# A transform and an expert layer on one core: the ramp reordered, filters split, weight roundings moved, products of zeros added, pieces of the body shifted

## The chip, the cores and the metric

The kernel runs on one core of a Trainium2 chip. Its time is the device time of one execution in microseconds. A profile is one execution; its span is mostly some 2 us below that execution's time. A product of 32-bit numbers shows as two records in these traces, so x8 in a line of PE is four products. Engines are called PE (tensor engine), PEld (its weight loads), DVE (vector engine), ACT (scalar engine), POOL (GpSimd) and SP (the engine that issues most of the transfers).

## The reference

```python
X = np.fft.rfft(x, axis=1)                      # x: 8 batches x 3008 positions x 256 channels
y = np.fft.irfft(X * (filt_r + 1j * filt_i), n=3008, axis=1)
h = y.reshape(24064, 256) @ w_in                # 256 x 2048
out = (h * (1.0 / (1.0 + np.exp(-h)))) @ w_out  # 2048 x 256
```

The weights arrive as 64-bit numbers. The kernel turns them into 32-bit ones on the chip; this is what "rounding" means below: 16 of them, two to a weight pair, each some five operations of DVE, two of ACT and two of POOL, and four more POOL operations after every second one.

## The kernel before

The transform of a batch goes through DRAM twice: stage 1 (products `pa`) stores d1; six groups load t2 from it, multiply (forward, `pb`), take the filter's product on DVE, add, multiply (inverse, `pc`), and store q into d2; stage 3 (`pd`) loads t4 from d2 and makes y. The expert products then run in 48 steps per batch (`px`, `pyz`, `acc`), and between them the next batch's transform is fed in piece by piece, by a list of steps and rounds. Only batch 0's transform has nothing to hide behind: it is the ramp.

```python
def stage1(u):
    t1 = tpool.tile([128, 2, 2, C], FP32, name=f"t1_{b}_{u}", tag="t")   # two buffers
    # ... products into two banks, evacuated by DVE and ACT, stored to d1 from POOL's queue

# the ramp
for u in range(8):
    part["load_x"](u)
nc.sync.dma_start(out=d_t, in_=d_dram.ap())
weights(0)
load_filters()                       # all 12 rows per partition, 3 MB
# ... sums and stage 1, eight pieces
part["load_t2"](0)
part["load_t2"](1)
nc.sync.dma_start(out=e_t, in_=e_dram.ap())
weights(1)
weights(2)
nc.sync.dma_start(out=wi_t, in_=wi_dram.ap())
rounded(0)
rounded(1)
for g in range(NG):
    part["forward"](g)
    # ... multiply and add, two halves each
    if g > 0:
        part["inverse"](g - 1)
    if g % 2 == 0:
        weights(3 + g // 2)
    rounded(2 + g)
part["inverse"](NG - 1)
part["load_t4"](0)
rounded(8)
rounded(9)
for g in range(4):
    part["stage3"](g)
# ... the other six roundings stand in steps 0 to 5, one each
```

The body's list of pieces, for batch b:

```python
put(at - 49, 0, part["load_x"], 0)              # at = 48 * b
for u in range(8):
    put(at + u - 48, 5, part["sums"], u)        # DVE
    put(at + u - 47, 3, part["stage1"], u)
```

Of the kernel before, what the change touches and what calls it, by code (L numbers as in the profile page):

```python
# [39 lines left out]
FP32 = mybir.dt.float32  # L40
# [97 lines left out]
def kernel(  # L138
# [47 lines left out]
    w_t = cpool.tile([128, 7, 2, NJP, 128], FP32)  # L186
    warm = cpool.tile([128, 1], FP32)
    bias_t = cpool.tile([128, 1], FP32)
    x_t = [xpool.tile([128, 2, 2, C], FP32, name=f"x{i}") for i in range(2)]

    def load_filters():
        for j in range(4):
            s0, tau = slot_residue(0, 0, j), (1 if j % 2 == 0 else -1)
            for half in range(2):
                off, t = (s0, tau) if half == 0 else (94 - s0, -tau)
                for k, filt in enumerate((filt_r, filt_i)):
                    p0 = 32 * j + 16 * half
                    nc.sync.dma_start(
                        out=f_t[k][p0:p0 + 16].rearrange("p g k c -> p (g k) c"),
                        in_=bass.AP(tensor=filt.tensor, offset=filt.offset + off * C,  # L200
                                    ap=[[94 * C, 16], [t * C, 2 * NG], [1, C]]))

    flip = [0]

# [20 lines left out]
    def spectral(b):  # L225
# [5 lines left out]
        def load_x(u):  # L231


            queue = nc.sync
            if b == 0:
                queue = (nc.sync, nc.scalar)[u % 2]
                if u in (0, 2):
                    xs["y"] = ypool.tile([128, 2, HALF], FP32, name=f"x_{b}_{u}", tag="y")
                if u < 4:
                    xs[u] = xs["y"][:, u % 2, 0:1024].rearrange("p (a n) -> p a n", a=2)  # L240
                elif u < 6:
                    xs[u] = t4pool.tile([128, 2, 2 * C], FP32, name=f"x_{b}_{u}", tag="t4")
                else:
                    xs[u] = x_t[u % 2]
                (nc.vector, nc.gpsimd)[u % 2].memset(xs[u][32:64], 0.0)
            else:
                xs[u] = x_t[u % 2]
            for h in range(2):
                for r0, nr in ((0, 32), (32, N1 - 32)):
                    queue.dma_start(  # L250
                        out=xs[u][64 * h + r0:64 * h + r0 + nr],
                        in_=bass.AP(tensor=x.tensor,
                                    offset=x.offset + (b * S + 32 * r0 + 4 * u + 2 * h) * C,
                                    ap=[[32 * C, nr], [32 * N1 * C, 2], [1, 2 * C]]))
# [14 lines left out]

        def stage1(u):  # L270
            ut = us.pop(u)
            t1 = tpool.tile([128, 2, 2, C], FP32, name=f"t1_{b}_{u}", tag="t")
            ps = [bank(b, f"pa_{b}_{u}_{h}") for h in range(2)]
            for par in range(2):
                for h in range(2):
                    rows = slice(64 * h, 64 * h + N1)
                    nc.tensor.matmul(out=ps[h][64 * par:64 * par + 64], lhsT=wf_t[rows, par],  # L277
                                     rhs=ut[rows, par], start=True, stop=True)
            for h in range(2):
                evac(t1[:, h], ps[h])  # L280
            for par in range(2):
                nc.gpsimd.dma_start(  # L282
                    out=d1[par].rearrange("s p n c -> (s p) n c")[:, 4 * u:4 * u + 4, :],
                    in_=t1[64 * par:64 * par + 2 * NS].rearrange("p h n c -> p (h n) c"))
# [31 lines left out]

        def add(g, k):
            z, pt = prods[g][k]
            eng = nc.vector if b > 0 else nc.gpsimd
            eng.tensor_tensor(out=z[:, 0], in0=z[:, 0], in1=pt[:, 1], op=ALU.subtract)  # L320
            eng.tensor_tensor(out=z[:, 1], in0=z[:, 1], in1=pt[:, 0], op=ALU.add)  # L321

        def inverse(g):
# [6 lines left out]
                        nc.tensor.matmul(out=ps[i][:, k, :], lhsT=e_t[rows, g, k, ri, :],  # L330
                                         rhs=zs[k][rows, ri, :], start=(ri == 0), stop=(ri == 1))
            for i in range(2):
                qt = qpool.tile([128, 2, C], FP32, name=f"q_{b}_{g}_{i}", tag="q")
                evac(qt, ps[i])
                for p in range(2):
                    a0 = p * NS + 2 * g + 12 * i
                    queue = nc.gpsimd if b > 0 else nc.scalar
                    queue.dma_start(out=d2[a0:a0 + 2, :, :].rearrange("s n c -> n s c"),  # L338
                                    in_=qt[64 * p:64 * p + 64, :, :])

# [36 lines left out]
    def plan(b, part):  # L377

        at = STEPS * b
        put(at - 49, 0, part["load_x"], 0)  # L380
        put(at - 49, 0, part["load_x"], 1)
        for u in range(8):
            put(at + u - 48, 5, part["sums"], u)
            put(at + u - 47, 3, part["stage1"], u)
        put(at - 39, 0, part["load_t2"], 0)
        put(at - 39, 0, part["load_t2"], 1)
        for g in range(NG):
            put(at + 3 * g - 37, 3, part["forward"], g)
            put(at + 3 * g - 37, 5, part["multiply"], g, 0)
            put(at + 3 * g - 36, 1, part["multiply"], g, 1)  # L390
            put(at + 3 * g - 36, 5, part["add"], g, 0)
            put(at + 3 * g - 35, 1, part["add"], g, 1)
            put(at + 3 * g - 35, 3, part["inverse"], g)
        put(at - 18, 5, part["load_t4"], 0)
        for g, step in enumerate((-16, -12, -8, -4)):
            put(at + step, 3, part["stage3"], g)
        plan_rest(b, part)
# [216 lines left out]
    def weights(jp):  # L614
        if wide:
            load_weights(jp)

    def rounded(j):
        if wide:
            round_weights(j)  # L620
        else:
            load_exact(j)


    nc.sync.dma_start(out=wf_t, in_=wf_dram.ap())
    nc.gpsimd.memset(bias_t, -896.0)
    part = spectral(0)
    for u in range(8):
        part["load_x"](u)
    nc.sync.dma_start(out=d_t, in_=d_dram.ap())  # L630
    weights(0)
    load_filters()
    for u in range(3):
        part["sums"](u)
    for u in range(8):
# [3 lines left out]
    part["load_t2"](0)  # L639
    part["load_t2"](1)  # L640
    nc.sync.dma_start(out=e_t, in_=e_dram.ap())
    weights(1)
    weights(2)
    nc.sync.dma_start(out=wi_t, in_=wi_dram.ap())
    rounded(0)
    rounded(1)
    for g in range(NG):
        part["forward"](g)
        for k in range(2):
            part["multiply"](g, k)  # L650
        for k in range(2):
            part["add"](g, k)
        if g > 0:
            part["inverse"](g - 1)
        if g % 2 == 0:
            weights(3 + g // 2)
        rounded(2 + g)
    part["inverse"](NG - 1)
    part["load_t4"](0)
    rounded(8)  # L660
    rounded(9)
    for g in range(4):
        part["stage3"](g)
    early[0] = None
    plan_rest(0, part)
    for b in range(1, B):
        plan(b, spectral(b))
    for k in range(6):
        put(k, 1, rounded, 10 + k)
        if k in (1, 3):  # L670
            put(k, 1, weights, 6 + k // 2)

    per = len(PAIRS) * 2

    stores = (((10, 1), (10, 5)), ((19, 5), (20, 1)), ((28, 5), (29, 1)), ((34, 1), (34, 5)),
              ((42, 1), (42, 5)), ((50, 1), (51, 1)))
    for pair in range(len(pairs)):
        pending.append((NJP * pair - 2 + (5 if pair % per == 3 else 1) / ROUNDS, 100,
# [54 lines left out]
```

## Time and profile before

| | before |
|---|---|
| median of 4 runs | 2746.07 us (2745.39 to 2747.09) |
| span of the profile | 2745.5 us |
| PE busy | 2630.5 us, 96% |
| first expert product starts | 146.43 us |
| steps 1 to 5 (one rounding each) | 42.94 us |
| a batch period in the body | 326.85 us |

PE is full in the body, so a gain can come from two places: the 146 us before the first expert product, and single waits in the body. The prediction below shows the lines that say so. In such a ramp the busy shares say little; a table of landmarks (the first product of each stage) and the chain of waits between two landmarks say which resource carries each stretch.

### The profile page before, as it was taken

What the parts mean: (1) busy time and instruction counts of PE and PEld (TensorE: products, weight loads), DVE (VectorE), ACT (ScalarE), POOL (GpSimd) and SP (SyncE); (2) the same over time, 40 slices, a digit from 0 to 9 for tenths busy, and PEclk for the clock granted to TensorE, in tenths of its full rate; (3) what the DMA queues carried; (4) which work ended last, traced back from release to release, by engine and by line L of the source; (5) the groups of instructions that cost most, each with busy time, mean ns of one, the idle gap of its engine ahead of it and who ended that gap; (6) DMA issues with size and microseconds to landing.
All of it is one profiled execution on the core that took longest, in us unless ns stands there. A gap on an engine that the chain in (4) does not pass through costs nothing.

```text
span 2745.5 us, 45764 instructions
## 1 busy us (share of the span) xinstructions
PE 2630.5 (96%) x17664; PEld 2198.8 (80%) x17664; DVE 1652.4 (60%) x3492; ACT 1098.9 (40%) x2994; POOL 506.0 (18%) x738
## 2 busy tenths in 40 slices
PE   2489999999999999999999999999999999999998
PEld 0368889788887888878887888878888788898987
DVE  3676655666556665666656665566655666555555
ACT  1244344433444334443444434444344433444443
POOL 2541210211111111112111121022111211110100
PEclk9789999999999999999999999999999999999999
DMA  9643221331214221332113312133121421110000
GB/s 176 192 125 79 49 46 32 88 79 40 46 37 105 65 50 23 71 85 68 35 33 82 81 47 44 35 82 85 39 47 31 107 65 43 32 27 20 9 16 15
DMA packets 187929, 166.94 MB, mean 61 GB/s; under 512 B 122176, under 2 KB 155584, under 8 KB 187456
## 3 DMA queue, kind: packets, MB, share of 16 engines
q1 hardware_dynamic: 165912, 111.89, 18.0%
q0 software_dynamic: 16256, 47.20, 6.8%
q10 hardware_dynamic: 5544, 4.93, 0.8%
q8 instruction: 138, 2.26, 0.3%
q14 instruction: 79, 0.65, 0.1%
HBM read 88.96 MB, written 74.97 MB: 60 GB/s over the span
## 4 chain that ended last, share of the span: by engine, by line
PE 90%; DVE 4%; DMA 2%; ACT 1%; issue 1%; ACTq 0%; SPq 0%; POOL 0%; DVEq 0%; POOLq 0%
PE acc L495 40%; PE px L439 24%; PE pyz L439 17%; PE pc L330 3%; PE pd L358 3%; PE pa L277 2%; PE pb L300 2%; DMA d<-t 1%; DVE g L410 1%; DVE u L265 1%; DMA x<-in_x_dram 1%; ACTq L338 0%; DVE z L321 0%; DMA raw<-in_moe_w_out_dram 0%; DVE z L320 0%
## 5 line engine op out<-in xcount | busy, mean ns | idle before, releaser
L495 PE MATMUL acc<-g,w_t 128*128 128x256 f32 (+1 forms) x5376 | 1512.5, 375 | 0.4 <-DVE g L410 0.4
L495 PEld LDWEIGHTS acc<-g,w_t 128*128 128x128 f32 x5376 | 1021.9, 190 | 115.6 <-DVE g L410 0.8
L410 DVE TENSOR_TENSOR g<-pyz,abc 128x256 f32<-128x256 f32 (+1 forms) x1152 | 478.2, 415 | 569.3 <-ACT abc L460 323.0
L410 DVE TENSOR_TENSOR g<-g 128x256 f32<-128x256 f32 (+3 forms) x1152 | 611.8, 531 | 196.6 <-ACT g L443 183.4
L439 PE MATMUL px<-ty,w_t 128*128 128x256 f32 (+1 forms) x2304 | 695.4, 383 | 3.5 <-ACT abc L454 2.9
L443 ACT ACTIVATE g<-g 128x256 f32<-128x256 f32 (+1 forms) x1152 | 472.8, 410 | 244.8 <-DVE g L410 244.8
L439 PEld LDWEIGHTS px<-ty,w_t 128*128 128x128 f32 x2304 | 420.5, 190 | 128.5 <-issue 71.0
L439 PE MATMUL pyz<-y,w_t 128*128 128x256 f32 (+1 forms) x1536 | 456.3, 379 | 10.9 <-DVE g L410 10.9
L410 POOL TENSOR_TENSOR s<-s 128x256 f32<-128x256 f32 (+1 forms) x329 | 266.4, 827 | 1022.2 <-DVE s L513 999.0
L439 PEld LDWEIGHTS pyz<-y,w_t 128*128 128x128 f32 x1536 | 282.0, 189 | 58.8 <-DVE g L410 20.1
L454 ACT COPY abc<-px 128x256 f32<-128x256 f32 (+1 forms) x384 | 141.2, 368 | 373.3 <-PE px L439 373.3
L443 ACT ACTIVATE g<-px 128x256 f32<-128x256 f32 (+1 forms) x384 | 145.8, 380 | 302.1 <-PE px L439 302.1
L460 ACT COPY abc<-px 128x256 f32<-128x256 f32 (+1 forms) x384 | 142.9, 372 | 285.2 <-PE px L439 284.9
L338 POOL DMA_DIRECT2D d<-q x168 | 99.3, 598 | 713.5 <-DVE q L208 705.6
L439 PE MATMUL px<-y,w_t 128*128 128x256 f32 (+1 forms) x768 | 226.2, 376 | 1.0 <-ACT y L210 1.0
L439 PE MATMUL pyz<-ty,w_t 128*128 128x256 f32 (+1 forms) x768 | 226.7, 377 | 0.0
L439 PEld LDWEIGHTS pyz<-ty,w_t 128*128 128x128 f32 x768 | 145.2, 190 | 19.0 <-DVE g L410 2.9
L439 PEld LDWEIGHTS px<-y,w_t 128*128 128x128 f32 x768 | 144.3, 190 | 19.6 <-ACT y L210 1.1
L447 ACT COPY abc<-px 128x256 f32<-128x256 f32 (+1 forms) x384 | 134.1, 349 | 1.3 <-PE px L439 1.3
L282 POOL DMA_DIRECT2D d<-t x128 | 65.6, 516 | 332.1 <-ACT abc L460 283.7
L330 PE MATMUL pc<-z,e_t 64*128 64x256 f32 x768 | 106.0, 413 | 16.0 <-POOL z L320 13.4
L208 DVE COPY y<-pd 128x376 f32<-128x376 f32 x64 | 51.7, 808 | 100.7 <-PE pd L358 100.7
(49 smaller groups left out, 1306.9 us busy)
## 6 DMA issues: line engine op xcount, KB each, us to landing
d<-t POOLq DMA_DIRECT2D x128, 192.0 KB, 3.0
t<-d SPq DMA_DIRECT2D x96, 256.0 KB, 3.9
t<-d SPq DMA_DIRECT2D x128, 192.0 KB, 3.9
d<-q POOLq DMA_DIRECT2D x168, 128.0 KB, 2.6
out_dram<-o SPq DMA_DIRECT2D x636, 32.0 KB, 1.8
x<-in_x_dram SPq DMA_DIRECT2D x120, 128.0 KB, 3.0
x<-in_x_dram SPq DMA_DIRECT2D x120, 60.0 KB, 2.9
raw<-in_moe_w_in_dram SPq DMA_DIRECT2D x16, 256.0 KB, 4.8
```

What stands on the lines that cost most here:

```text
L277: nc.tensor.matmul(out=ps[h][64 * par:64 * par + 64], lhsT=wf_t[rows, par], rhs=ut[rows, par], start=True, stop=True)
L282: nc.gpsimd.dma_start(out=d1[par].rearrange("s p n c -> (s p) n c")[:, 4 * u:4 * u + 4, :], in_=t1[64 * par:64 * par + 2 * NS].rearrange(" ...
L330: nc.tensor.matmul(out=ps[i][:, k, :], lhsT=e_t[rows, g, k, ri, :], rhs=zs[k][rows, ri, :], start=(ri == 0), stop=(ri == 1))
L338: queue.dma_start(out=d2[a0:a0 + 2, :, :].rearrange("s n c -> n s c"), in_=qt[64 * p:64 * p + 64, :, :])
L358: nc.tensor.matmul(out=ps[h][c0:c0 + 64, cb, i, :], lhsT=t4s[g][rows, i, 128 * cb + c0:128 * cb + c0 + 64], rhs=wi_t[rows, :], start=True, ...
L410: eng.tensor_tensor(out=out, in0=in0, in1=in1, op=op)
L439: nc.tensor.matmul(out=out, lhsT=w_t[:, c, 0, jp], rhs=rhs, start=start, stop=True, skip_group_check=True)
L443: nc.scalar.activation(out=g[:, k, 0:n], in_=g[:, k, 0:n] if src is None else src, func=AFT.Silu)
L447: nc.scalar.copy(out=sums[:, 0, 0:n], in_=xo)
L454: nc.scalar.copy(out=sums[:, 1, 0:n], in_=xo)
L460: nc.scalar.copy(out=sums[:, 2, 0:n], in_=xo)
L495: nc.tensor.matmul(out=acc[pair][i][:, h, 0:n], lhsT=w_t[:, c, 1, jp], rhs=g[:, k, 0:n], start=(jp == 0 and h == 0), stop=last, skip_group ...
```

## The change

Its intent: start the groups earlier by loading only the filter rows that the first two groups need, let stage 1 run ahead on six tiles, take the roundings out of the groups' chain, keep PE's clock up with products of zeros where it would stand still, and move a few pieces of the body off a crowded spot. The core of the diff (renamings and unchanged lines cut):

```diff
-    load_filters()
+    load_filters(0, 4)
 ...
+            if b > 0 or u < 2 or u > 5:
                 t1 = tpool.tile([128, 2, 2, C], FP32, name=f"t1_{b}_{u}", tag="t")
+            elif u < 4:
+                t1 = typool.tile([128, 2, 2, C], FP32, name=f"t1_{b}_{u}", tag="ty")
+            else:
+                t1 = us["t1"][:, u - 4]
 ...
-            eng = nc.vector if b > 0 else nc.gpsimd
+            eng = nc.vector if b > 0 or (g == NG - 1 and k == 0) else nc.gpsimd
 ...                                             # q: second half from another pool (4 tiles)
+    def idle(n):                                # n products of 128x128 zeros by 128x256 zeros
+            nc.tensor.matmul(out=ps[:, 0:256], lhsT=zero_t[:, 0:128], rhs=zero_t, ...)
+    idle(10)                                    # ahead of stage 1
 ...
-    weights(1)
-    weights(2)
+    idle(26)                                    # ahead of forward(0)
     for g in range(NG):
         part["forward"](g)
+        idle(4)
+        if g == 0:
+            load_filters(4, 2 * NG)
+        if g < 3:
+            weights(1 + g)
         ...
+        if 2 <= g < NG - 1:
+            rounded(g)
         if g > 0:
             part["inverse"](g - 1)
-        if g % 2 == 0:
-            weights(3 + g // 2)
-        rounded(2 + g)
     part["inverse"](NG - 1)
+    weights(4)
     part["load_t4"](0)
-    rounded(8)
-    rounded(9)
+    idle(22)
+    for j in range(5, 9):
+        rounded(j)
+        if j == 5:
+            weights(5)
 ...
-    for k in range(6):
-        put(k, 1, rounded, 10 + k)
+    for j in range(9, NJ):                      # seven roundings in steps 0 to 5, two in step 5
+        put(*((j - 9, 1) if j < NJ - 1 else (5, 5)), rounded, j)
 ...
-        put(at - 49, 0, part["load_x"], 0)
+        put(at - 51, 0, part["load_x"], 0)
-            put(at + u - 48, 5, part["sums"], u)
+            put(at + u - (48 if u else 49), 5, part["sums"], u)
 ...                                             # last group one step later, additions of
 ...                                             # group 4 and the stores of pair 2 later
```

More of the change, by code (lines that the diff above doesn't have):

```diff
@@ L188, with load_filters @@
     bias_t = cpool.tile([128, 1], FP32)
+    zero_t = cpool.tile([128, 256], FP32)
     x_t = [xpool.tile([128, 2, 2, C], FP32, name=f"x{i}") for i in range(2)]
-    def load_filters():
+    def load_filters(first, last):
         for j in range(4):
@@ L198, in load_filters @@
                     nc.sync.dma_start(
-                        out=f_t[k][p0:p0 + 16].rearrange("p g k c -> p (g k) c"),
-                        in_=bass.AP(tensor=filt.tensor, offset=filt.offset + off * C,
-                                    ap=[[94 * C, 16], [t * C, 2 * NG], [1, C]]))
+                        out=f_t[k][p0:p0 + 16].rearrange("p g k c -> p (g k) c")[:, first:last],
+                        in_=bass.AP(tensor=filt.tensor, offset=filt.offset + (off + t * first) * C,
+                                    ap=[[94 * C, 16], [t * C, last - first], [1, C]]))
     flip = [0]
@@ L236, in load_x @@
                 queue = (nc.sync, nc.scalar)[u % 2]
+                if u == 0:
+                    us["t1"] = gpool.tile([128, 2, 2, 2, C], FP32, name="t1_g", tag="g")
                 if u in (0, 2):
@@ L271, in stage1 @@
             ut = us.pop(u)
-            t1 = tpool.tile([128, 2, 2, C], FP32, name=f"t1_{b}_{u}", tag="t")
+            if b > 0 or u < 2 or u > 5:
+                t1 = tpool.tile([128, 2, 2, C], FP32, name=f"t1_{b}_{u}", tag="t")
+            elif u < 4:
+                t1 = typool.tile([128, 2, 2, C], FP32, name=f"t1_{b}_{u}", tag="ty")
+            else:
+                t1 = us["t1"][:, u - 4]
             ps = [bank(b, f"pa_{b}_{u}_{h}") for h in range(2)]
@@ L332, in inverse @@
             for i in range(2):
-                qt = qpool.tile([128, 2, C], FP32, name=f"q_{b}_{g}_{i}", tag="q")
+                if b > 0 or i == 0:
+                    qt = qpool.tile([128, 2, C], FP32, name=f"q_{b}_{g}_{i}", tag="q")
+                else:
+                    qt = opool.tile([128, 2, C], FP32, name=f"q_{b}_{g}_{i}", tag="o")
                 evac(qt, ps[i])
@@ L336, in inverse @@
                     a0 = p * NS + 2 * g + 12 * i
-                    queue = nc.gpsimd if b > 0 else nc.scalar
+                    queue = nc.gpsimd if b > 0 or (g == NG - 1 and i == 0) else nc.scalar
                     queue.dma_start(out=d2[a0:a0 + 2, :, :].rearrange("s n c -> n s c"),
@@ L379, in plan @@
         at = STEPS * b
-        put(at - 49, 0, part["load_x"], 0)
-        put(at - 49, 0, part["load_x"], 1)
+        put(at - 51, 0, part["load_x"], 0)
+        put(at - 51, 0, part["load_x"], 1)
         for u in range(8):
-            put(at + u - 48, 5, part["sums"], u)
+            put(at + u - (48 if u else 49), 5, part["sums"], u)
             put(at + u - 47, 3, part["stage1"], u)
@@ L386, in plan @@
         put(at - 39, 0, part["load_t2"], 1)
-        for g in range(NG):
-            put(at + 3 * g - 37, 3, part["forward"], g)
-            put(at + 3 * g - 37, 5, part["multiply"], g, 0)
-            put(at + 3 * g - 36, 1, part["multiply"], g, 1)
-            put(at + 3 * g - 36, 5, part["add"], g, 0)
-            put(at + 3 * g - 35, 1, part["add"], g, 1)
-            put(at + 3 * g - 35, 3, part["inverse"], g)
+        for g, step in enumerate((-37, -34, -31, -28, -25, -21)):
+            late = 4 if g == 4 else 0
+            put(at + step, 3, part["forward"], g)
+            put(at + step, 5, part["multiply"], g, 0)
+            put(at + step + 1, 1, part["multiply"], g, 1)
+            put(at + step + 1, 5 + late, part["add"], g, 0)
+            put(at + step + 2, 1 + late, part["add"], g, 1)
+            put(at + step + (3 if late else 2), 3, part["inverse"], g)
         put(at - 18, 5, part["load_t4"], 0)
@@ L622, in rounded @@
             load_exact(j)
+    def idle(n):
+        ps = xps.tile([128, 512], FP32, name="idle", tag="x")
+        for _ in range(n):
+            nc.tensor.matmul(out=ps[:, 0:256], lhsT=zero_t[:, 0:128], rhs=zero_t, start=True, stop=True)
     nc.sync.dma_start(out=wf_t, in_=wf_dram.ap())
+    nc.vector.memset(zero_t, 0.0)
     nc.gpsimd.memset(bias_t, -896.0)
     part = spectral(0)
+    idle(10)
     for u in range(8):
@@ L641 @@
     nc.sync.dma_start(out=e_t, in_=e_dram.ap())
-    weights(1)
-    weights(2)
-    nc.sync.dma_start(out=wi_t, in_=wi_dram.ap())
     rounded(0)
     rounded(1)
+    idle(26)
     for g in range(NG):
         part["forward"](g)
+        idle(4)
+        if g == 0:
+            load_filters(4, 2 * NG)
+            nc.sync.dma_start(out=wi_t, in_=wi_dram.ap())
+        if g < 3:
+            weights(1 + g)
         for k in range(2):
@@ L667 @@
         plan(b, spectral(b))
-    for k in range(6):
-        put(k, 1, rounded, 10 + k)
-        if k in (1, 3):
-            put(k, 1, weights, 6 + k // 2)
+    for j in range(9, NJ):
+        put(*((j - 9, 1) if j < NJ - 1 else (5, 5)), rounded, j)
+        if j in (11, 13):
+            put(j - 9, 1, weights, j // 2 + 1)
     per = len(PAIRS) * 2
-    stores = (((10, 1), (10, 5)), ((19, 5), (20, 1)), ((28, 5), (29, 1)), ((34, 1), (34, 5)),
+    stores = (((10, 1), (10, 5)), ((19, 5), (20, 1)), ((30, 1), (30, 5)), ((34, 1), (34, 5)),
               ((42, 1), (42, 5)), ((50, 1), (51, 1)))
```

## The prediction

> **What bounds the kernel now.** I read the page's forty slices first, then busy time by stretch, then the chain of waits for each stretch. From the slices (68.6 us each) the reader sees that the tensor engine (PE) is full from the fourth slice on, and that the DMA engines are full only in the first:
>
> ```profile
> PE   2489999999999999999999999999999999999998
> DMA  9643221331214221332113312133121421110000
> ```
>
> So the span is a ramp (the first batch's transform, before the expert products can start), a PE-bound body, and a short tail. Busy time by stretch (length, then PE, PEld, DVE, ACT, POOL busy, then granted clock, DMA share, GB/s) splits the ramp where its work changes:
>
> ```profile
> 0.00:60.00 60.00, 18.16 (x64) 4.77 (x64) 19.35 (x31) 6.21 (x11) 11.01 (x23) 1.00 0.96 175
> 60.00:126.00 66.00, 31.04 (x288) 18.62 (x288) 42.94 (x70) 12.84 (x21) 39.06 (x55) 0.86 0.71 204
> 126.00:146.43 20.43, 8.21 (x256) 7.71 (x257) 9.45 (x15) 6.37 (x9) 9.66 (x13) 0.50 0.50 124
> 146.43:158.70 12.27, 11.16 (x30) 7.37 (x30) 9.18 (x19) 4.40 (x11) 1.41 (x2) 0.62 0.35 94
> 158.70:201.72 43.02, 38.26 (x185) 26.55 (x187) 38.53 (x69) 20.45 (x52) 24.20 (x32) 1.00 0.44 131
> ```
>
> To 60 us DMA is at 0.96 and no engine is at a third. From 60 to 126 (the six groups) nothing is full: that is a chain. From 126 to 158.7 the granted clock is at or near half. From 158.7 each step takes 8.6 us (43.02 / 5), against 7.26 us once the roundings are over. The chain of waits names what holds the first two stretches:
>
> ```profile
> 26.86 31.83 DMA d<-t x4
> ...
> 82.79 0.61 DVE q L208
> 83.42 0.67 ACTq L338
> 84.12 0.61 ACTq L338
> 84.78 0.60 ACT q L210
> 85.39 0.58 ACTq L338
> 86.02 0.62 ACTq L338
> 86.73 0.64 ACT work L579
> 87.40 0.69 DVE work L583
> ...
> 134.89 1.99 PE pd L358 x63
> ...
> 223.50 1.08 PE pd L358 x64
> ```
>
> First, the stores of stage 1: two tiles hold its output, so each evacuation waits until an earlier store has landed, and those stores share the DMA engines with 3 MB of filters. Then a loop of about 8.9 us per group: DVE's multiplications, a q copy, four store issues on ACT, and the rounding of a weight pair, whose halves hop DVE, ACT, DVE. The last two lines are the same products cold and warm: 1.99 against 1.08 us.
>
> In the body only one wait recurs. All PE waits from 200 us to the end:
>
> ```profile
> PE pyz L439 <- DVE g L410: 8.4, 12, 1.0
> ```
>
> At 813.32 the chain shows DVE with sums(0) of the next batch for 1.70 us, between the drains of a pair; PE loses 0.97 us. A batch period is 326.8 us with PE busy 325.3.
>
> [...] the clock column says 1.00 before 60 us, where stage 1's 128x512 products last 1,073 ns on average against 615 later. [...] stage-1 stores take up to 18.1 us to land while filters are queued, 2.8 us when they are not. [...] In the groups the shift of a rounding takes 0.94 us beside GpSimd's additions, 0.42 without.
>
> **The change part by part.**
>
> (a) Filters. Only 4 of 12 rows (groups 0 and 1) are loaded before t2; 2,048 of 3,072 KB move behind forward(0). While mainly filters moved, at 45 to 55 us, DMA ran at 133 to 135 GB/s: 2.1 MB / 0.134 MB per us = 15.6 us. Stage 1 also gets six tiles instead of two, so its stores are issued early; but DMA was already full, so I credit no more for that. Stage-1 stores end at 63.6 - 15.6 = 48 us. From request of t2 to full use took 5.3 us (63.66 to 68.98), so forward(0) starts at about 53 instead of 69.
>
> (b) The groups. Roundings leave groups 0, 1 and 5 and stand behind the additions in 2 to 4; q has four tiles. ACT's share then is one copy and four issues, 3.0 us, DVE's 2.4 (four products) + 0.7. The chain that made 8.9 us is gone, and what remains is what DMA must bring: the order on the queue is table e 1.57 MB, t2(2), filters 2.1 MB, weights 1, t2(3), weights 2, t2(4), weights 3, t2(5). Filters at 0.134 MB per us again 15.6 us. The rest is 1.57 + 4 x 0.52 + 3 x 1.05 + five groups' stores 2.6 = 9.4 MB; DMA ran at 242 to 273 GB/s from 85 to 95 us, so 36 us. Sum 52 us: t2(5) is in at about 100. Then forward 1.1, multiply 2.4, add 1.4 (DVE and GpSimd side by side), inverse 1.9, copy 0.7: the last q on DVE at about 107.5, before at 125.74. Gain 18.
>
> (c) From there to the first expert product: before 146.43 - 125.74 = 20.7 us. Store, landing and t4 load took 9.1 us and stay. The 22 products of zeros start about 1 us ahead of the q copy and take 9.5 us warm (0.43 each), so they end about as t4 arrives. Stage 3 then runs warm, but its third and fourth pieces still wait for a t4 tile to come free and be loaded (about 4.5 us), and four roundings at 3.4 us = 13.6 us lie on DVE. I get 18.5. Gain 2.
>
> (d) The first step runs warm: 12.3 us becomes 8.6. Gain 3.7.
>
> (e) For batch 1, sums(0) now stands ahead of step 0 in DVE's order, and its x load is issued only after the last t4 load; landing about 6 us later it blocks DVE for some 2 us. Cost 2.
>
> (f) Nine roundings stand before the steps instead of ten; the seventh in steps 0 to 5 costs 1.34 us (8.6 - 7.26), say 1.5.
>
> (g) In the body sums(0) goes a step earlier, where DVE is at 4.5 of 7.26 us. Six batches x 1.4 us = 8.4; I credit 7.5, as 1.3 us of DVE work might collide elsewhere.
>
> The other products of zeros (10 at the start, 26 before forward(0), 4 per group) lie in PE waits: 26 x 0.43 = 11 us warm, 22 cold, against a wait of some 25 us. They cost nothing and buy little, since those stretches are DMA's.
>
> Sum: 18 + 2 + 3.7 - 2 - 1.5 + 7.5 = 27.7, so 2745.9 - 27.7 = about **2718 us**.
>
> **The rivals.**
> 1. DMA doesn't bind in the groups. For it: before, rates of 359 to 370 GB/s were reached at 70 to 80 us. Then six groups at about 6 us follow from the compute side, and the last q is at 53 + 38 = 91: 16 us better, 2702.
> 2. The moved loads hurt fully: filters go slow beside t2 and the d2 stores, multiply(2) waits for all of them, and weight loads delay t2(3) to t2(5). Then the groups end near 120 and the total is about 2731. For it: [...] t2(3) now stands behind 3 MB. Against it: total bytes are unchanged.
> 3. The zeros get in the way. If PE is cold when the 22 begin, [...] any misfit with t4's arrival is added: 2 to 4 us. If they never warm it, 22 x 0.86 = 19 us delay stage 3 by 9 us: 2727.
> 4. The stall of (g) only moves: the body gives 0 instead of 7.5: about 2725.
>
> **Range and chances.** A gain over 2% needs 55 us, that is a first product at 91 us less what the body gives; the bytes that must move forbid it even under rival 1. A loss needs a new wait of 80 us. The range is rivals 1 and 2 with what the smaller terms may add: 2703 to 2731. Chances: faster 0.02, same 0.975, slower 0.005.
>
> **What would show it.** In the changed profile: the first forward product at about 53 us (above 60 proves (a) wrong); filters landing near 75 us and DMA share above 0.9 through the groups (below 0.8 favours rival 1); the last q copy at 107; stage 3's 64 products at 1.1 us instead of 1.99; the first expert product at 126; DVE waiting for x before step 0; the batch period near 325.5 and PE's 8.4 us of waits almost gone. The prediction is wrong if forward(0) doesn't come earlier, or if warm PE shortens the groups much more than the bytes allow.

## The result, and the profile after

The changed kernel takes 2723.43 us (median of 4 runs, 2719.87 to 2725.17), the one before 2746.07. The ratio is 0.9916, with a 95% interval of 0.9898 to 0.9933. Ratios here are the mean time of one kernel's runs over that of the other's of the same rounds, so they are not quite the ratio of the medians. The predicted 2718 us is 5 us off, inside its range. The profiled execution was the quickest of the four (span 2718.1 us), so the ledger below, made from the two traces, adds up to 27.4 us where the medians differ by 22.6.

The slices of the changed kernel (67.95 us each):

```profile
PE   7689999999999999999999999999999999999998
DMA  9733121421224211332122312132121421110000
```

PE fills the first slice now, but a good part of that is products of zeros, so a busy share can no longer be read as progress. Busy time by stretch, cut at the landmarks (length, then PE, PEld, DVE, ACT, POOL, granted clock, DMA share, GB/s):

```profile
0.00:42.19 42.19, 34.40 (x139) 20.17 (x140) 24.84 (x40) 8.57 (x14) 18.39 (x33) 0.88 0.90 237
42.19:60.00 17.81, 15.09 (x150) 10.04 (x150) 5.66 (x9) 0.58 (x1) 5.60 (x8) 0.90 0.92 220
60.00:80.00 20.00, 3.23 (x33) 1.25 (x34) 7.02 (x11) 1.94 (x3) 4.55 (x6) 0.57 1.05 196
80.00:104.60 24.60, 21.39 (x156) 13.57 (x156) 18.34 (x29) 4.35 (x7) 14.53 (x18) 0.86 0.72 195
104.60:127.78 23.18, 16.53 (x298) 14.57 (x297) 18.29 (x25) 8.88 (x13) 15.64 (x18) 0.78 0.77 187
127.78:138.82 11.04, 9.20 (x30) 5.84 (x30) 9.01 (x17) 3.93 (x10) 4.87 (x6) 0.84 0.25 61
```

From 60 to 80 us no engine is busy for more than 7.02 of the 20 us and DMA is full (1.05): the groups stand still for bytes. After that DMA is at 0.72. The ledger, from the landmarks of both traces (forward(0) is the start of its bulk, after both halves of t2 have landed; "last q" is the end of the last q copy on DVE; step 1 starts with the first `pa` after the first expert product, step 6 with the sixth):

| stretch | before, us | after, us | difference | predicted |
|---|---|---|---|---|
| to forward(0) | 68.98 | 42.19 | -26.8 | -16 |
| groups, to last q | 56.76 | 62.41 | +5.6 | -2 |
| to first expert product | 20.69 | 23.18 | +2.5 | -2.2 |
| step 0 | 12.28 | 11.04 | -1.2 | -1.7 |
| steps 1 to 5 | 42.94 | 47.89 | +4.9 | +1.5 |
| step 6 to stage-3 piece 4 | 21.78 | 21.78 | 0 | 0 |
| body, to the last stage-3 piece | 2336.87 | 2324.11 | -12.8 | -7.5 |
| rest | 185.2 | 185.5 | +0.3 | 0 |

The sum came out nearly as predicted, but of the six stretches for which a change was predicted only step 0 came near it. The chain of waits of the changed kernel through the groups (start, length, what):

```profile
57.68 3.87 DMA filt<-in_filt_r_dram
61.56 8.82 DMA filt<-in_filt_r_dram
70.41 7.26 DMA t<-d
...
79.76 3.71 PE idle L641 x8
83.47 1.09 PE pc L338 x8
```

The early start is paid back: group 2 waits for the filters that were moved out of the way, group 3 for a t2 that stands behind them. And four products of zeros, run cold in 3.71 us, lie on the chain ahead of an inverse product. From 77.7 to 106.7 us the chain holds no transfer any more. How much of the wait is the filters' is in the waits from 40 to 110 us (who waited for what: us in total, times, longest):

```profile
DVE z L320 <- DMA filt<-in_filt_r_dram: 17.2, 1, 17.2
```

In the body PE's waits after 200 us have shrunk from the 8.4 us that the prediction shows to the following and one more of 0.4 us, which the kernel before has too:

```profile
PE pd L369 <- DMA t<-d: 1.0, 2, 0.7
```

### The profile page after: what moved, and what is told of

It reads as the page before. It is cut to its first block, busy times and chain, and to the rows that moved or that the text cites. A ratio compares the mean times of both kernels' runs of the same rounds, so it can differ in the third digit from the quotient of the medians. Undisturbed runs are those within 1.5% of the kernel's fastest.

```text
span 2718.1 us, 46118 instructions
## 1 busy us (share of the span) xinstructions
PE 2659.3 (98%) x17828; PEld 2230.4 (82%) x17828; DVE 1655.2 (61%) x3495; ACT 1098.9 (40%) x2994; POOL 506.4 (19%) x738
## 4 chain that ended last, share of the span: by engine, by line
PE 92%; DMA 3%; DVE 2%; SPq 1%; issue 1%; ACT 1%; ACTq 0%; DVEq 0%
PE acc L508 41%; PE px L452 25%; PE pyz L452 18%; PE pc L338 3%; PE pd L369 3%; PE pa L285 2%; PE pb L308 2%; DMA t<-d 1%; DMA x<-in_x_dram 1%; DVE g L423 1%; SPq L199 1%; DMA filt<-in_filt_r_dram 0%; SPq L546 0%; DVE u L268 0%; DMA e_t<-e_tbl 0%
## 5 line engine op out<-in xcount | busy, mean ns | idle before, releaser
L452 PEld LDWEIGHTS px<-y,w_t 128*128 128x128 f32 x768 | 144.2, 190 | 22.6 <-issue 3.0
L338 PE MATMUL pc<-z,e_t 64*128 64x256 f32 x768 | 98.4, 395 | 3.5 <-POOL z L328 1.5
```

The source lines that it names most:

```text
L338: nc.tensor.matmul(out=ps[i][:, k, :], lhsT=e_t[rows, g, k, ri, :], rhs=zs[k][rows, ri, :], start=(ri == 0), stop=(ri == 1))
L452: nc.tensor.matmul(out=out, lhsT=w_t[:, c, 0, jp], rhs=rhs, start=start, stop=True, skip_group_check=True)
```

## The experiments

Twelve runs (the changed kernel again and eleven variants), all correct. The theory after reading the two traces: both the filter split and the six tiles bring forward(0) early, the bytes then hold the groups, so the real gains are the roundings' places and the body's schedule, and the rest of the change costs. The rival: the early start and the warm array are what pays. Landmarks in us from one trace each:

| run | median, us (range) | ratio to before | first forward product | last q | first expert product | steps 1 to 5 |
|---|---|---|---|---|---|---|
| before | 2746.07 | | 67.2 | 125.7 | 146.4 | 42.9 |
| after | 2723.43 (2719.87 to 2725.17) | 0.9916 | 41.2 | 104.6 | 127.8 | 47.9 |
| after again | 2722.68 (2722.32 to 2723.58) | 0.9917 | 42.1 | 105.4 | 129.6 | 45.9 |
| no zeros | 2718.47 (2717.32 to 2719.91) | 0.9902 | 42.6 | 102.3 | 126.3 | 46.6 |
| filters whole | 2716.65 (2713.68 to 2719.07) | 0.9892 | 56.5 | 101.9 | 126.2 | 46.7 |
| two tiles | 2727.89 (2725.62 to 2729.39) | 0.9935 | 48.9 | 111.0 | 135.8 | 46.0 |
| body only | 2738.50 (2736.93 to 2739.93) | 0.9977 | 66.2 | 125.7 | 147.3 | 43.0 |
| sums only | 2742.34 (2741.30 to 2745.30) | 0.9992 | 65.2 | 124.2 | 144.9 | 43.0 |
| ten roundings ahead | 2723.13 (2721.93 to 2724.16) | 0.9922 | 41.5 | 104.4 | 132.9 | 43.0 |
| reordered | 2717.41 (2716.85 to 2718.07) | 0.9900 | 40.7 | 103.5 | 125.9 | 43.0 |
| roundings as before | 2731.22 (2730.90 to 2733.43) | 0.9947 | 42.4 | 115.8 | 139.0 | 43.0 |
| no zeros in groups | 2722.34 (2721.64 to 2723.36) | 0.9914 | 42.8 | 102.3 | 128.9 | 47.9 |
| combined | 2715.83 (2714.67 to 2717.01) | 0.9889 | 56.4 | 105.9 | 126.4 | 43.1 |
| combined 2 | 2720.45 (2718.33 to 2722.09) | 0.9904 | 56.8 | 104.8 | 129.9 | 43.3 |

**The changed kernel once more.** No edit.

> The changed kernel once more, timed beside the others. Its four runs so far spread from 2719.9 to 2725.2 us with mean granted clocks of 0.989 to 0.986, while the kernel before spreads by under 2 us. If the scatter comes from how long the tensor engine runs at half clock in the ramp, the runs here should again spread over 4 to 6 us and the slower ones should show the lower mean clock; if it was one chip's chance, they should agree within 2 us. Median 2722 to 2725.

The median was as expected, the spread was not: 1.3 us here. Both chips together give 2719.9 to 2725.2, so differences under some 2 us between kernels of different calls are not used below. The clock theory of the scatter isn't borne out: this trace has a mean granted clock of 0.990 and is 3 us longer than the first, which has 0.989 (within the first four runs the slower ones did have the lower clock, 0.986 against 0.989). Single stretches scatter as well: here step 0 takes 12.39 us, not 11.04.

**Without zeros.**

```diff
-    idle(10)
-    idle(26)
-        idle(4)
-    idle(22)
```

> The changed kernel without any product of zeros (all 62 of them taken out). Prediction's view (they cost nothing and buy little): within 3 us of the changed kernel, 2720 to 2727. Rival (they are what keeps the array warm, and warm stretches are on the path): 5 to 12 us slower, 2728 to 2735, with stage 1, the forward and inverse products and stage 3 at about twice their warm durations. Second rival (they stand in the way, as the group of 22 that ends at 113.6 us, and the 4 between forward and inverse that took 3.8 us cold): 2 to 5 us faster.

The second rival is right: 4.2 us faster than the changed kernel on the same chip, with ranges that do not touch (2717.3 to 2719.9 against 2722.3 to 2723.6). The zeros do warm the array: the first stage-1 products, in the trace of the changed kernel with zeros ahead of them and then in that without:

```profile
8.29 1.68 PE L285 MATMUL pa<-u,wf_t 47*64 47x512 f32 x8 [0.67 <-DVE u L268]
```

```profile
8.33 2.58 PE L285 MATMUL pa<-u,wf_t 47*64 47x512 f32 x8 [8.33 <-DVE u L268]
```

These four products take 1.68 us behind zeros and 2.58 us without. But nothing waits for them: stage 1 is held by x, by copies and by stores (in the changed kernel, to 42 us: DVE waits 4.9 us for x, PE 1.4 for a copy, ACT and DVE 2.8 for stores), so forward(0) starts only 0.6 to 1.8 us earlier with zeros (42.2 and 43.4 against 43.9), and the last q comes 2.3 to 3.1 us later with them (104.6 and 105.4 against 102.3). The chain of the changed kernel above suggests the reason, and "no zeros in the groups" below bears it out for the last q: the four zeros stand in PE's order ahead of an inverse product, and DVE's next multiplication waits for that inverse to free its z tile (5.6 us in all; 3.9 in "no zeros in the groups"). Here warmth was worth nothing to an engine that waited anyway, and the products that made it stood in the way.

**Filters whole before t2.**

```diff
-    load_filters(0, 4)
+    load_filters(0, 2 * NG)
 ...
-            load_filters(4, 2 * NG)
```

> The changed kernel with all filter rows loaded before t2, as in the kernel before. If splitting the filters is what brings the first forward product from 67 to 41 us, it comes back to 50 to 57 us. The groups then no longer wait 17 us for filters at group 2. If the bytes bound the groups, the last q copy comes at nearly the same time as in the changed kernel (104.6 us), within 4 us, and the total is within 5 us of it (2720 to 2728). Rival: the split is worth its full 16 us in the end too: 2735 to 2740.

The idea in the title of the change, the split of the filters, costs some 6 us: without it forward(0) starts 15.6 us later (57.75 us), and still the last q is 2.7 us earlier and the kernel takes 2716.65 us against 2722.68, which is faster than the 2720 to 2728 expected. (Its four runs lie at 2714, twice, and at 2719, twice; all are faster than every run of the changed kernel, and the profile is of one at 2719.) With whole filters no wait for them is left. What holds the groups then, in two stretches of this run (columns as above):

```profile
80.00:90.00 10.00, 8.10 (x56) 5.04 (x56) 6.52 (x10) 2.02 (x4) 8.15 (x12) 0.66 0.92 269
90.00:102.00 12.00, 9.99 (x78) 6.41 (x75) 9.35 (x17) 2.41 (x4) 4.92 (x7) 0.86 0.52 147
```

To 90 us DMA (0.92, 269 GB/s) still sets the pace, then DVE's 9.35 of 12 us. The same bytes have to come in either way, and here it was better to have the filters first.

The run also shows what the tiles do, since it has six of them and the old order of loads. From 20 to 40 us, before and then in this run:

```profile
20.00:40.00 20.00, 5.17 (x22) 1.19 (x16) 3.69 (x6) 1.17 (x2) 2.01 (x4) 1.00 1.08 222
```

```profile
20.00:40.00 20.00, 17.74 (x78) 12.06 (x71) 10.65 (x18) 4.94 (x8) 10.36 (x18) 0.82 1.06 308
```

(The clock of 1.00 in the first line is no measurement: the clock records of that trace begin at 87.6 us.) The DMA share is the same, 1.08 and 1.06, but the rate is 222 against 308 GB/s, so a full share is not yet a full rate. With tiles free, the stores of stage 1 join in early and the stage is done 11.2 us sooner (forward(0) at 57.75 instead of 68.98).

**Two tiles for stage 1.**

```diff
-            if b > 0 or u < 2 or u > 5:
+            if True:                        # t1 always from the pool of two
```

> The changed kernel with stage 1 writing to two tiles again instead of six. My prediction gave the extra tiles nothing; the first forward product came 11 us earlier than predicted, so I now think they are worth about that at that point: it should start at 49 to 54 us here instead of 41. By the end of the groups part should be taken up by the shorter wait for filters: total 0 to 10 us slower, 2723 to 2733. If the tiles are worth nothing, all landmarks stay within 2 us of the changed kernel.

Forward(0) and forward(1) of this run:

```profile
48.91 1.62 PE L306 MATMUL pb<-t,d_t 64*32 64x256 f32 x32
52.39 1.09 PE L306 MATMUL pb<-t,d_t 64*32 64x256 f32 x32
```

The bulk of forward(0) (the third of its 32 records) starts at 49.45 us, where the prediction, which had credited the split of the filters alone, has 53. So the 26.8 us of the early start are 19.5 from the split (68.98 to 49.45; with up to 1.8 from the zeros) and 7.3 from the tiles (49.45 to 42.19). Taken in the other order they are 11.2 from the tiles ("filters whole") and 15.6 from the split. What DVE waits for stage-1 stores to free a tile, up to 69 us, in the kernel before, in this run, and in the run with whole filters:

```profile
DVE t L208 <- DMA d<-t: 34.7, 5, 14.5
```

```profile
DVE t L209 <- DMA d<-t: 15.0, 4, 7.9
```

```profile
DVE t L209 <- DMA d<-t: 1.7, 1, 1.7
```

At the end two tiles cost 5.2 us (2727.89 against 2722.68). Of the two ways to start early, the tiles, which let stores use a DMA rate that lay idle, keep 5.2 of their 7.3 us; the split, which only moves a load behind another use, costs more than it brings.

**The body's schedule alone**, on the kernel before.

```diff
-        put(at - 49, 0, part["load_x"], 0)      # and 1
+        put(at - 51, 0, part["load_x"], 0)      # and 1
-            put(at + u - 48, 5, part["sums"], u)
+            put(at + u - (48 if u else 49), 5, part["sums"], u)
 ...                                             # last group, additions of group 4, stores of pair 2
```

> The kernel before with only the schedule of the body changed (x loads and sums(0) earlier, the last group a step later, the additions of group 4 later, the stores of pair 2 later); ramp as before. In the changed kernel the body (from the first stage-3 piece in the steps to the last) is 12.7 us shorter than before. If that comes from the schedule alone, this runs at 2732 to 2736 us (about 0.5% faster than before). If part of it comes from the ramp (another alignment of loads), it gains only 4 to 9 us: 2737 to 2742.

The body, from the fourth piece of stage 3 to its last, takes 2324.1 us, 12.8 less than before and the same as in the changed kernel: the whole gain of the body is the schedule's. The total, 2738.5 us, misses 2732 to 2736, the range for a gain from the schedule alone, because step 0 takes 16.56 us instead of 12.28. In the waits of step 0 stands why:

```profile
DVE u L265 <- DMA x<-in_x_dram: 3.1, 1, 3.1
PE pyz L441 <- DVE g L412: 5.1, 4, 3.5
```

That is term (e) of the prediction: batch 1's x is asked for behind the last t4 load, and DVE, which needs it before step 0's drains, holds PE for 3.5 us. In the changed kernel the wait is absent: there x is requested at 123.35 us, and DVE, busy with roundings and copies, comes to it only at 129.30.

**Sums alone**, on the kernel before: `load_x` at -51 and `sums(0)` at -49, and nothing else of the schedule.

> The kernel before with only the x loads and sums(0) a step or two earlier. My prediction credited the body's whole gain to this (0.97 us of wait in each of six batches, 7.5 us in all): 2737 to 2740. The trace shows a second wait of 0.43 us per batch near the last group, and each wait also makes the next product longer (0.70 instead of 0.43 us), so the two waits together come to about 2.3 us per batch; this one alone should give about 1.4 to 1.6 us in each of six batches, 8 to 10 us less up to 2 us for the wait for x before step 0: 2736 to 2740. If it gives all of the body's gain it is at 2733 to 2735.

The body takes 2329.4 us, 7.5 less than before, which is what the prediction credited to this move. The x wait is the same (3.2 us; step 0 takes 16.73 us), so the total of 2742.34 misses the expectation in the same way (its ratio, 0.998 to 1.0005, is not clear of none). What is left of PE's waits after 200 us:

```profile
PE pyz L439 <- DVE g L410: 3.3, 7, 0.7
```

One of the seven, of 0.7 us, lies ahead of the body; six of 0.43 us are left in it, where before there were twelve with 8.4 us: six of 0.97 at sums(0), and these six near the last group. In the chain of the kernel before, the product after such a wait took 0.70 us and the next ones 0.43, so a wait costs its restart of 0.27 us too: 6 x (0.97 + 0.27) = 7.4 us, measured 7.5. For the second kind, which the other moves of the schedule remove, the same sum gives 6 x (0.43 + 0.27) = 4.2 us; measured are 5.3 between this run and "body only", and the 1.1 us between them are within the scatter of the body, which differs by up to 2.8 us between the traces that have the new schedule. The prediction took all 8.4 us for the waits at sums(0).

**Ten roundings ahead of the steps**, one a step after that.

```diff
-    for j in range(5, 9):
+    for j in range(5, 10):
 ...
-        put(*((j - 9, 1) if j < NJ - 1 else (5, 5)), rounded, j)
+        put(j - 10, 1, rounded, j)
```

> The changed kernel with ten roundings before the steps instead of nine, so that no step holds two. In the changed kernel step 5 with two roundings takes 13.0 us instead of about 8.6, with a wait of 2.64 us and then half clock. If that is the seventh rounding's price, the steps give back 4 us here. A fifth rounding before stage 3's evacuations costs up to 4.6 us (the four there take 18.5 us). So the total is -3 to +3 us, 2720 to 2726, and the pieces show: steps 1 to 5 at 43 us instead of 47.9, first expert product at 130 to 133 us instead of 127.8.

As expected: steps 1 to 5 go back to 43.0 us, the first expert product comes 3 to 5 us later (132.9), and the total doesn't move, 2723.13. The two roundings in step 5 cost 3 to 5 us, and so does one more rounding between the groups and stage 3. The wait in the changed kernel, from 139 to 200 us, and a product after it in the chain (0.43 us at full clock):

```profile
PE px L452 <- ACT g L456: 2.6, 1, 2.6
```

```profile
183.32 0.85 PE acc L508 x2
```

The 2.64 us wait was followed by products at half rate (0.85 us each against 0.43) until 185.8 us. In "after again" the same wait of 2.64 us was not: its granted clock stays at 1.00 through that stretch and steps 1 to 5 take 45.9 us. From 181.0 to 186.7 us, in the changed kernel and then in "after again" (columns as above; 0.70 and 1.00 are the granted clocks):

```profile
181.00:186.70 5.70, 5.57 (x16) 4.02 (x16) 5.15 (x8) 1.60 (x5) 4.61 (x6) 0.70 0.19 56
```

```profile
181.00:186.70 5.70, 3.05 (x12) 2.11 (x12) 4.82 (x10) 2.84 (x7) 2.58 (x4) 1.00 0.51 139
```

Six traces have this wait. In three of them it was followed by half rate: the changed kernel, "no zeros" (a granted clock of 0.74 from 178.0 to 184.5 us) and "no zeros in groups" (products of 0.85 us again). In "after again" it was not; what decides this was not shown. Steps 1 to 5 take 45.9 us without the fall of the clock and 46.6 to 47.9 with it, so most of the price of the double step is there without the half clock.

**Roundings reordered**, filters still split.

```diff
         if g == 0:
+            weights(1)
             load_filters(4, 2 * NG)
 ...                                             # roundings 2, 3 behind inverse(0) in group 1,
 ...                                             # 4, 5 in groups 3, 4; 6 to 9 after the groups
-    for j in range(5, 9):
+    for j in range(6, 10):
 ...                                             # weight pair 5 asked for after stage3(0); one rounding a step
```

> A version meant to be better: weight pair 1 is loaded ahead of the second part of the filters and rounded while the vector engine waits for them (17 us idle in the changed kernel); roundings 4 and 5 stand in groups 3 and 4, 6 to 9 after the groups, one per step from 10 on; weight pair 5 is requested after stage 3's first piece instead of before its second t4 tile. If the vector engine's roundings are what holds the groups after 84 us and stage 3, and the double rounding what costs step 5: last q at 98 to 102 us, first expert product at 118 to 124, no 13 us step: 2708 to 2716. If the bytes hold the groups throughout, only the double rounding and the t4 tile are gained: 2716 to 2720.

2717.41 us: better than the changed kernel by some 5 us, outside the range hoped for and inside the one that was expected if the bytes hold the groups. The last q comes at 103.5 us, 1.1 to 1.9 us earlier than in the changed kernel: DVE fills the wait for filters with two roundings, but 10.2 us of it remain (put down to the table that is loaded right behind the filters). The gain is in the first expert product (125.9) and in steps without a double rounding (43.0); step 0, with 14.45 us, gives 2 to 3.4 us of it back.

**Roundings in their old places**, all else changed.

```diff
+    weights(1)                                  # before the groups, and 2; then 3 + g // 2
 ...
-        if 2 <= g < NG - 1:
-            rounded(g)
         if g > 0:
             part["inverse"](g - 1)
+        rounded(2 + g)
 ...                                             # 8 and 9 after the groups; one rounding a step
```

> The changed kernel with the roundings and the weight loads of the ramp back in the places of the kernel before (two ahead of the groups, one behind the inverse of each group, two after them, one in each of the steps 0 to 5); filters split, six tiles and products of zeros stay. So far the split of the filters took 3 us away from the gain at the last q copy, the six tiles gave 6, the zeros cost 2, and the gain there is 21 us: by difference the roundings should give about 20 us. Then the last q copy comes at 118 to 126 us instead of 104.6, the time from it to the first expert product is back at about 20 us, no step takes 13 us: total 2732 to 2740. If the bytes bound the groups anyway, it comes at 105 to 112 us and the total is 2716 to 2726.

The last q is at 115.8 us, 10.4 to 11.2 later than in the changed kernel's two traces, and the time 2731.22, some 8 us more. The expected time began at 2732 and the expected last q at 118, so both were nearly met. With split filters, six tiles and zeros all in place, this undoes more of the ramp's gain than any other single edit. But the edit moves more than roundings: weight pairs 1 and 2 are asked for ahead of the moved filters, whose last one here lands at about 74.6 us on the chain (70.4 in the changed kernel), rounding 7 holds up a store (see "combined 2"), and the double step is gone. How the 8 us divide among these was not run.

**No zeros in the groups** (`idle(4)` alone removed).

> The changed kernel without the four products of zeros in each group alone; the 10, 26 and 22 stay. Without any zeros the kernel was 4.2 us faster. If it is those in the groups that cost (the inverse waits behind them, and the multiplications wait for the inverse to free z), this gains 2 to 5 us over the changed kernel: 2718 to 2721, last q at 101 to 103 us. If it is the 22 that delay stage 3, this stays within 1.5 us of the changed kernel, 2721 to 2724.

The last q comes at 102.34 us, the same as without any zeros, so the four per group are what delays it. The total, 2722.34 us, doesn't follow: the first product of stage 3 comes 1.8 us later than in the run without zeros and the first expert product 2.5 us later. The 22 zeros behind the groups, which this run has and that one hasn't, are not the reason; they end before stage 3 can start:

```profile
101.55 9.76 PE L641 MATMUL idle<-zero_t 128*128 128x256 f32 x44
112.93 0.28 PE L369 MATMUL pd<-wi_t,t 48*64 48x47 f32 x2 [1.62 <-DMA t<-d]
```

PE is done with them at 111.31 us and waits 1.62 us more for its t4, which is asked for at 109.68 us, 1.5 us later than without zeros (108.15). Why, is not known. In the changed kernel they end at 113.60 us, 0.23 us after the t4 has landed.

**Combined**: no zeros, whole filters, six tiles; weights 1, 2 and 3 asked for in groups 0, 1 and 3; one rounding in each of groups 1 to 4; 6 to 9 after the groups; pair 5 after stage3(0); then one rounding a step; sums(0) of batch 1 in its old place.

> What the runs so far recommend, together: all filters before t2, no products of zeros, six tiles, roundings 2 to 5 in groups 1 to 4, 6 to 9 after them and one per step from 10 on, weight pair 3 requested behind t2(5), pair 5 behind stage 3's first piece, sums(0) of batch 1 in its old place (its wait for x cost 4.3 us before the first step in the run of the body alone), the body's schedule new. Whole filters 6 us, no double rounding 3 to 5, the x wait 3 to 4, zeros up to 3, less up to 4 for a tenth rounding ahead of the steps: 2704 to 2713. If the bytes bound the groups whatever the order, 2711 to 2717.

2715.83 us (2714.67 to 2717.01), the lowest of all: 31 us under the kernel before and 7 us under the changed one, but not the 2704 to 2713 hoped for; it lies in the range expected if the bytes hold the groups in any order. It cannot be told from "filters whole" (2716.65) and "reordered" (2717.41): three different edits end within 2 us of each other. Here the products of the inverse are cold (a mean of 572 ns against 435 in the changed kernel), and the last q is at 105.9.

**Combined 2**: whole filters; zeros only in the groups, roundings 2 to 4 in groups 2 to 4 and 5 behind inverse(4) in group 5; weight pairs 1 to 3 as in the changed kernel, the rest as in "combined".

> A second combination, from the run with whole filters, which had the earliest last q copy (101.9 us): only the four products of zeros per group stay (the inverse took 2.0 us there, 3.5 to 4.3 in the combination without any), roundings 2 to 4 in groups 2 to 4, rounding 5 behind group 5's additions, 6 to 9 after the groups, one per step from 10 on; pair 5 requested behind stage 3's first piece, sums(0) of batch 1 in its old place. Last q at 102 to 104 us, first expert product 20.5 us later, 11.5 us for step 0, 43 us for steps 1 to 5: total 2709 to 2715. If the products of zeros in the groups are not worth it, or the rounding behind group 5 delays the last copies by its whole length, 2715 to 2719.

2720.45 us, 5 us above the first range expected and 1.5 above the second. The chain behind the last q of this run:

```profile
104.28 1.61 POOL w_t L604 x2
...
109.87 0.61 POOL d L349
```

The last group's first store of q is issued from POOL's queue in the changed kernel. A rounding placed ahead of it ends in POOL work, so the store is issued only at 109.87 although its q was copied by 104.8 (in the changed kernel 104.60, and the issue at 104.89), and stage 3 starts 11.5 us after the last q. In "roundings in their old places", where a rounding stands there too, it is also 11.5 us; in the other runs 7.9 to 9.5, but for 10.6 in "no zeros in groups". A queue is a place in an order, also for transfers (here an issue at 109.87 instead of 104.89 us).

## Why the prediction was right or wrong

The time was right to 5 us (2718 predicted, 2723.43 measured), and within 2% as expected. Several steps were not, and their errors cancel: that the sum came so near is luck.

- **(a), the early start: -26.8 instead of -16 us.** The step that failed is "DMA was already full, so I credit no more for that". The tiles gave another 7.3 us (11.2 with whole filters), because a DMA share of 1.08 at 222 GB/s was not full; 308 GB/s went through at 1.06. The split was sized too small as well: with two tiles it gave 19.5 us where 15.6 were computed. The load of t2 was requested at 44.75 us instead of 63.66, so 2.1 MB had cost 18.9 us, which is 0.11 MB per us and not the 0.134 of the stretch that was read.
- **(b), the groups: +5.6 instead of -2 us,** so that the last q came at 104.6 where 107.5 was predicted. That bytes would hold the groups was right for their first part only: the DMA share was 0.92 and 1.05 to 80 us, but 0.72 after that, below the 0.8 that was to favour rival 1. The part that the bytes set came out near: forward(5) began 49.1 us after forward(0) (51.0 in "after again"), and the sum has 47. The step that failed is the tail behind it, from t2(5) to the last q: 13.3 us (11.0) instead of 7.5. DVE begins multiply(5) only at 97.2 us, behind rounding 4 (92.2 to 96.7), and the inverse after it takes 3.71 us (2.34) instead of 1.9. So most of what was won beyond the sum ahead of the groups was lost in them. DVE's single wait for filters, 17.2 us, is what rival 2 described, and "filters whole" shows its price: 6 us, far less than the rival's 13.
- **(c), to the first expert product: +2.5 instead of -2.2 us.** Four roundings at 3.4 us were assumed; they took 18.55 us (104.51 to 123.06), 4.6 each: the first waits 2.8 us for ACT, and in the others DVE's operations last longer beside POOL (the shift 0.95 to 0.97 us, in the first 0.42). t4(1) stood behind weight pair 5, which the sum left out; in "reordered", where it doesn't, the bulk of the second piece starts at 115.3 us instead of 118.8. In the chain of the changed kernel:

```profile
112.77 5.91 DMA t<-d
118.82 2.00 PE pd L369 x63
```

  The t4 of the second piece takes 5.91 us to land, and the piece runs cold again (2.00 us); the 22 zeros warmed only the first (1.15 us for its 64 records). Rival 3 was wrong about these 22; the zeros that did get in the way are those in the groups.
- **(d), step 0 warm: -1.2 instead of -3.7 us** (the table of the ledger nets it with (e)). PE had gone cold behind the late t4 (granted clock 0.50 from 117.9 to 131.0 us) and began step 0 so; its granted clock over the step is 0.84, better than the 0.62 of before but not 1. In "after again" step 0 took 12.39 us and nothing was gained.
- **(e), x for batch 1: 0 instead of +2 us in the changed kernel,** since its DVE was late for its own reasons; in "body only", where DVE was not, step 0 took 4.3 us longer, and in "roundings in their old places" DVE waits 2.2 us for x and step 0 takes 14.67.
- **(f), the seventh rounding: +4.9 us in one trace, +2.9 in the other, instead of +1.5.** The term took a mean cost per rounding. Two in one step make a wait of 2.64 us, and half clock after it in the changed kernel (0.70 from 181.0 to 186.7 us) but not in "after again" (1.00); "ten roundings ahead" has neither.
- **(g), the body: -12.8 instead of -7.5 us.** The step that failed is "Six batches x 1.4 us": it put waits of two kinds down to sums(0). Its own waits are six of 0.97 us, which with their restarts are the 7.5 that the move alone gives (that the credited 7.5 is just this is luck, since no restart was counted); the other six went with the plan's other moves, for 5.3.
- **The zeros: "cost nothing" was wrong,** they cost 4.2 us. It is true that their time lies in waits at the start and before stage 3; in the groups they lie ahead of products that were due, and the last q comes 2.3 to 3.1 us later with them.

Of the two theories the experiments were made for, the first holds: split and zeros cost (6 and 4.2 us), the places of the roundings and of their weight loads (8 us) and the body (12.8 us) gain. Against it, the tiles, which belong to the early start, do pay 5.2 us. Each of these is what undoing one piece of the changed kernel does, or adding it to the one before; they add up to some 16 of the 22.6 us, and the pieces' effects on each other were not run.

Rival 1 (the compute side decides, last q at 91) fell: no run came below 101.9. Rival 4 (the body gives nothing) fell with "body only". Two slips in the prediction's readings changed nothing: the stage-1 products are 47x512 and not 128x512, and the clock column before 60 us is no measurement there.

What stays open: why taking out the groups' zeros alone brought the last q forward but not the total; whether they cost anything with whole filters (the last q came at 101.9 us with them in "filters whole" and at 105.9 without in "combined", but there the roundings moved too); and how the 8 us of "roundings in their old places" divide.

## What to carry to other kernels

An early start is worth what the next stretch doesn't take back, so find out what holds that stretch before buying it: here, of 27 us ahead of the groups, the tiles' 7 left 5 at the end and the split's 16 cost 6, while moving roundings and their weight loads off the groups' chain gave about 8 us and shifting a few pieces in a full body gave 12.8. Judge a full DMA by its GB/s as well as by its share (222 and 308 GB/s here, at 1.08 and 1.06), and put extra work (roundings, warming products, stores) only where nothing due stands behind it in the same queue. When a prediction is a sum of terms, compare the terms, since a right sum can hide several wrong ones.
